# The first softplus stage in tile pairs over two token blocks, the second in halves, and a leaner attention front

## The chip, the core and the metric

The kernel runs on one core of one Trainium2 chip. The time is the device time of one execution, in microseconds (us). The engines are TensorE (PE, matmuls; PEld is its weight load), VectorE (DVE), ScalarE (ACT), GpSimd (POOL) and SyncE (SP, which issues most DMAs).

## The reference

A gated linear attention over 2 batches of 768 tokens (8 heads of 48) feeds a softplus layer, and that feeds four weighted ReLU experts:

```python
mag = np.sqrt(a_re * a_re + a_im * a_im)
scale = np.minimum(mag, 0.999) / (mag + 1e-06)
a_re_n, a_im_n = (a_re * scale, a_im * scale)
for t in range(S):
    new_re = ar * S_re - ai * S_im
    new_im = ar * S_im + ai * S_re
    kv = np.einsum('bhd,bhe->bhde', k[:, :, t], v[:, :, t])
    S_re, S_im = (new_re + kv, new_im)
    y[:, :, t] = np.einsum('bhd,bhde->bhe', q[:, :, t], S_re)
...
h = x @ w_in                                   # 1536 x 384 by 384 x 2048
g = np.maximum(h, 0.0) + np.log1p(np.exp(-np.abs(h)))
x = g @ w_out                                  # 2048 x 384
...
for e in range(E):                             # 4 experts, 384 -> 1024 -> 384
    h = np.maximum(x @ w1[e], 0.0)
    out += p[:, e:e + 1] * (h @ w2[e])
```

w_in and w_out come as 64-bit floats, the rest as 32-bit floats.

## The kernel before, in words

`fast_path` does the whole computation; `general_path` stands behind a flag and doesn't run on these inputs.

**Stages.** Twelve stages k, six for each batch: in a batch, stages 0 and 1 are the two halves (1024 columns each) of the softplus layer, stages 2 to 5 the experts. `ORDER` (line 40) gives their order; the last six are computed in another way (`FAST`) and aren't touched by the change. A matmul operand is split into a high and a low part (float32r), and a product takes three matmuls.

**A step.** `step` (line 366) takes a stage k, a block of tokens blk and one of eight column tiles f. `first` (236) runs nine h matmuls (line 232), and then, for softplus, ACT's Abs, Exp and Ln and DVE's line 250; in stage 0 two column tiles share one 512-wide tile. `second` (265), one step later, splits the result into two g tiles (lines 275 and 276, or 285 and 286). `third` (291), `LAG` = 3 steps later, runs nine y matmuls (314). Stage 0 has three blocks of 256 tokens (24 steps), the others two of 384 (16 steps). A block goes through all eight f before the next. At the last f of a block the sum is closed: stage 0 copies it to `Yt` (326), stage 1 adds it (331) and splits it into X (332, 333). PSUM has tiles by tag: `h` (2 banks), `a` (3), `y` (a tile of two banks) and `z` (1).

**Weights.** `weights` (160) loads the tiles A (first layer) and B (second layer) of four weight pairs a stage. In stages 0 and 1 a tile comes as two halves of 64-bit numbers: `load2` issues two loads on SP, `conv` runs `join` (69: lines 70 to 72 on DVE, which make 32-bit floats), `part` (179: ACT's 181 and DVE's 182) and stores the joined half to DRAM for batch 1 (line 200, on SP). Raw tiles have four buffers, slots nine (`NR`); three tiles of stage 1 have spare buffers (`early`), which later give their room to X of batch 1 (`swap`).

**Attention.** Six pairs of 128-token chunks, three a batch; the text counts pairs 1 to 6 and chunks 1 to 12 (the code counts n from 0). Batch 0 is pairs 1 to 3. For a pair: `squares` (543), `ratio` (549), `arctan`, `logmag` (558), then prefix sums by matmul (`prefix`, `wrap`, `level`), whose last row goes to the next chunk by a DMA on SP and an addition on POOL (`carry` 613, line 574), then `trig`. For a chunk (`s3_units`, 655): `decay` (653), `prep` (665), `turn` (transposes 674, copies 675), `score` (683, 684), `mix` (699), `state` (710, 714, 716) and `done`, which writes X (721, 722). Pairs 1 and 2 mix into bank z, pair 3 into an a bank. Block i of stage 0 needs pair i + 1.

**The order of the work.** Units are put at positions (`put`, 760), stage 0 at 0 to 24, stage 1 at 24 to 40, and are issued in order of position (`run`). A scheduler may still move instructions ahead where their inputs are ready. The weights of stage 0 stand at -5.2 + 1.6 n (n = 0 to 7: A and B of weight pair 1, then of 2, 3, 4), those of stage 1 at 8.3 + 2.3 n, later where a slot comes free later. `back(0)` (chunks 1 and 2) stands at -7.9 to -3.8, `back(1)` (3 and 4) at -0.7 to 6.3, `back(2)` (5 and 6) at 8.3 to 15.7 (lines 863 to 868).

```python
put([lambda k=k, blk=blk, f=f: step(k, blk, f) for blk in range(blks) for f in range(FH)], base[m], base[m + 1])
...
        pos, gap = -5.2 + 1.6 * n, 0.4
```

## Time and profile before

| | us |
|---|---|
| median of 3 runs | 737.89 |
| lowest and highest run | 735.72, 739.29 |
| span of the profiled execution | 736.2 |
| its own device time | not listed apart from the span |
| PE busy | 703.0 (95%) |
| DVE busy | 584.7 (79%) |
| ACT busy | 487.0 (66%) |
| POOL busy | 33.3 (5%) |

Busy is the time in which an engine has an instruction under way. Matmuls overlap, so that a listed matmul is longer than what it adds, and PE's busy time is an upper value. The chain that ended last is 70% PE, 10% DVE, 9% DMA and 8% ACT.

### The profile page before, as it was taken

Reading aid. Unit: us, or ns where it says so; the run is one execution under the profiler, and the core shown is the slowest. Engines: PE = TensorE matmul, PEld = TensorE weight load, DVE = VectorE, ACT = ScalarE, POOL = GpSimd, SP = SyncE. Lnnn points to the kernel's source line nnn. Section 1 sums busy time; section 2 is a strip of 40 time slices with the busy share of each in tenths; the row PEclk is TensorE's granted clock in tenths of the full one; section 3 lists DMA queues with packets and bytes.
Section 4 is the critical chain, followed back from the end, with each engine's and each line's share of the span. In section 5 each row is a group of like instructions: output and inputs, shape, how many; then the busy total and the mean of one; then the engine's idle time right before and its main releaser. Section 6 shows DMA issues by size and latency. Waiting matters only on the chain.

```text
span 736.2 us, 13313 instructions
## 1 busy us (share of the span) xinstructions
PE 703.0 (95%) x5171; PEld 676.2 (92%) x5171; DVE 584.7 (79%) x1150; ACT 487.0 (66%) x898; POOL 33.3 (5%) x31
## 2 busy tenths in 40 slices
PE   1688999999999999999999999999999999999996
PEld 0477899999899999999999999999999999999996
DVE  6999999955875854648888779988788899988963
ACT  7887886878896856345686666555556667666640
POOL 1132010000111011000000000000000000000000
PEclk9699999999999999999999999999999999999998
DMA  7655666721211420121022130213454445554501
GB/s 264 195 175 170 230 190 195 228 84 44 75 55 59 122 81 2 59 86 44 23 86 65 29 102 21 87 44 98 128 159 146 137 151 172 151 172 140 172 32 69
DMA packets 36486, 83.56 MB, mean 113 GB/s; under 512 B 4544, under 2 KB 13376, under 8 KB 36416
## 3 DMA queue, kind: packets, MB, share of 16 engines
q1 hardware_dynamic: 36128, 82.35, 35.5%
q8 instruction: 42, 0.69, 0.4%
q10 hardware_dynamic: 288, 0.30, 0.1%
q14 instruction: 28, 0.23, 0.1%
HBM read 73.95 MB, written 8.65 MB: 112 GB/s over the span
## 4 chain that ended last, share of the span: by engine, by line
PE 70%; DVE 10%; DMA 9%; ACT 8%; issue 2%; POOL 1%; SPq 0%; ACTq 0%; POOLq 0%; DVEq 0%
PE y L314 21%; PE h L232 18%; PE z L314 9%; PE px L425 7%; PE pv L425 3%; PE tp L674 2%; DMA rawB<-in_w_dram 2%; DMA chkw<-in_w_in_dram 2%; PE pc L425 2%; PE sp L683 2%; PE yps L699 2%; DMA chki<-in_a_im_dram 1%; PE ya L359 1%; PE sps L710 1%; DVE fA L72 1%
## 5 line engine op out<-in xcount | busy, mean ns | idle before, releaser
L232 PE MATMUL h<-X,A 128*128 128x384 f32 (+1 forms) x936 | 176.1, 329 | 2.5 <-ACT A L181 0.8
L232 PEld LDWEIGHTS h<-X,A 128*128 128x128 f32 x936 | 153.4, 188 | 5.8 <-issue 1.6
L314 PE MATMUL y<-B,g 128*128 128x384 f32 x744 | 150.0, 335 | 0.0
L314 PEld LDWEIGHTS y<-B,g 128*128 128x128 f32 x744 | 131.1, 188 | 0.5 <-issue 0.2
L314 PE MATMUL y<-g,B 128*128 128x384 f32 (+1 forms) x504 | 91.0, 315 | 0.3 <-ACT g L285 0.3
L314 PE MATMUL z<-B,g 128*128 128x384 f32 x372 | 84.7, 334 | 0.0
L314 PEld LDWEIGHTS y<-g,B 128*128 128x128 f32 x504 | 79.3, 189 | 1.9 <-ACT g L285 0.6
L314 PEld LDWEIGHTS z<-B,g 128*128 128x128 f32 x372 | 66.3, 188 | 0.0
L247 ACT ACTIVATE e<-h 128x384 f32<-128x384 f32 (+1 forms) x60 | 30.8, 513 | 37.3 <-PE h L232 36.3
L250 DVE SCALAR_TENSOR_TENSOR e<-h,e 128x384 f32<-128x384 f32 (+1 forms) x60 | 34.9, 581 | 21.0 <-ACT e L103 20.1
L255 DVE SCALAR_TENSOR_TENSOR g<-h,g 128x384 fp32r<-128x384 f32 x32 | 17.7, 554 | 28.2 <-ACT g L254 28.2
L103 ACT ACTIVATE e<-e,b_one 128x384 f32<-128x384 f32 (+1 forms) x60 | 38.2, 637 | 1.3
L103 ACT ACTIVATE e<-e 128x384 f32<-128x384 f32 (+1 forms) x60 | 32.8, 547 | 1.3
L425 PE MATMUL px<-X,sA 128*128 128x384 f32 x144 | 33.7, 339 | 0.0
L425 PE MATMUL px<-XC,sA 128*128 128x384 f32 x144 | 33.0, 337 | 0.1
L314 PE MATMUL z<-g,B 128*128 128x384 f32 x144 | 32.9, 335 | 0.0
L674 PE MATMUL tp<-ident,QK 128*96 128x128 f32 x192 | 27.3, 290 | 5.9 <-DVE QK L665 5.0
L674 PEld LDWEIGHTS tp<-ident,QK 128*96 128x96 f32 x192 | 22.4, 133 | 10.0 <-DVE QK L665 6.2
L254 ACT ACTIVATE g<-h 128x384 fp32r<-128x384 f32 x32 | 15.6, 487 | 21.3 <-PE h L232 21.1
L286 DVE TENSOR_TENSOR g<-e,g 128x384 fp32r<-128x384 f32 x48 | 26.7, 555 | 3.8 <-ACT g L285 3.0
L490 ACT CAST B<-rawB 128x768 fp32r<-128x768 f32 x24 | 20.0, 835 | 14.1 <-DMA rawB<-in_w_dram 7.6
L490 ACT CAST A<-rawA 128x384 fp32r<-128x384 f32 (+1 forms) x48 | 20.3, 457 | 11.6 <-DMA rawA<-in_w_dram 9.2
(204 smaller groups left out, 1424.4 us busy)
## 6 DMA issues: line engine op xcount, KB each, us to landing
rawA<-in_w_dram SPq DMA_DIRECT2D x32, 384.0 KB, 3.0
rawB<-in_w_dram SPq DMA_DIRECT2D x32, 384.0 KB, 3.1
rawA<-in_w_in_dram SPq DMA_DIRECT2D x16, 384.0 KB, 3.7
rawB<-in_w_out_dram SPq DMA_DIRECT2D x16, 384.0 KB, 3.8
chkw<-in_w_in_dram SPq DMA_DIRECT2D x16, 384.0 KB, 3.5
chkw<-in_w_out_dram SPq DMA_DIRECT2D x16, 384.0 KB, 3.3
qk<-in_qkv_dram SPq DMA_DIRECT2D x12, 384.0 KB, 3.3
v<-in_qkv_dram SPq DMA_DIRECT2D x12, 256.0 KB, 3.1
```

What stands on the lines that cost most here:

```text
L103: i = nc.scalar.activation(out_, in_, fn, **kw)
L232: nc.tensor.matmul(ps, wt[:, p, kk, o:o + P], XB[b][:, q, kk, tok], start=(n == 0), stop=(n == 3 * KT - 1))
L247: nc.scalar.activation(t, h, AF.Abs)
L250: nc.vector.scalar_tensor_tensor(t, h, 0.0, t, ALU.max, ALU.add)
L254: nc.scalar.activation(g[:, 0, :], h, AF.Relu)
L255: nc.vector.scalar_tensor_tensor(g[:, 1, :], h, 0.0, g[:, 0, :].bitcast(F32), ALU.max, ALU.subtract)
L286: nc.vector.tensor_tensor(g[:, 1, :], t, g[:, 0, :].bitcast(F32), ALU.subtract)
L314: mm = nc.tensor.matmul(ys[j], l_, r_, start=(opens and n == 0 and not mate), stop=(closes and n == 2), skip_group_check=k == 0)
L425: nc.tensor.matmul(ps, lt[:, p, li, :], rhs, start=(start and n == 0), stop=(stop and n == 2), skip_group_check=True)
L490: nc.scalar.copy(hi, src)
L674: nc.tensor.transpose(tp[:96, hh, :], src[:, hf * 4 + hh, :], ident)
L683: nc.tensor.matmul(sp[:, hh, :], kT[:, hh, :], qT[:, hh, :], start=True, stop=True)
```

## The change

- Stage 0 goes by `SEQ0`: weight pairs 1 and 2 over blocks 0 and 1, then these over block 2, then weight pair 3 over the three blocks, then 4. All three blocks are open at once: blocks 0 and 1 share the y and z banks, block 2 takes two of the three a banks.
- Stage 1 runs the first four f over both blocks, then the last four. It closes four times instead of twice; the first two closes only add to Y.
- Weight tiles of stages 0 and 1 stand at later positions, all in the nine slots; the spare buffers go, and X of batch 1 has its room from the start.
- Attention pairs 2 and 3 stand earlier: `back(1)` at -2.5 to 1.9, `back(2)` at 4.4 to 7.9, what leads to them at -8 to -2.6 and 0.2 to 4.2.
- The squares of pairs 2 and 3 are added on DVE instead of POOL.
- `ratio` loses the clamp of the slope; `logmag` keeps twice the log magnitude, with its small correction out of a biased Exp, and loses a scaling pass; `decay` halves the value in its Exp scale.

```diff
--- before.py
+++ after.py
@@ -40,6 +40,8 @@
 ORDER = (0, 1, 2, 3, 6, 7, 4, 5, 8, 9, 10, 11)
 AT = {k: m for m, k in enumerate(ORDER)}
 FAST = ORDER[6:]
+SEQ0 = ([(blk, 2 * j + i) for j in range(2) for blk in range(2) for i in range(2)] + [(2, f) for f in range(4)]
+        + [(blk, 2 * j + i) for j in range(2, 4) for blk in range(3) for i in range(2)])
 HALF = 4
 NORM_SPREAD = 2.0 ** 14
 
@@ -84,8 +86,7 @@
     att_ctx = ExitStack()
     att = att_ctx.enter_context(tc.tile_pool(name="att", bufs=1))
     psum = ctx.enter_context(tc.tile_pool(name="psum", bufs=1, space=PSUM))
-    early_ctx = ExitStack()
-    early = early_ctx.enter_context(tc.tile_pool(name="early", bufs=1, side="right"))
+    xb = ctx.enter_context(tc.tile_pool(name="xb", bufs=1, side="right"))
 
     NOSYNC = mybir.DependencyInfo(mybir.DependencyClass.NoSync, mybir.DependencyReason.DATA)
     tabs = {"load": None, "since": []}
@@ -129,6 +130,7 @@
     b_hpi = column("b_hpi", math.pi / 2.0)
     b_one = column("b_one", 1.0)
     b_tiny = column("b_tiny", 1e-37)
+    b_2eps = column("b_2eps", math.log(2e-6))
     b_mid = column("b_mid", -(2.0 ** 30))
     pr = const.tile([P, NTOK // P, NE], F32, name="pr")
     psm = const.tile([P, NTOK // P, 1], F32, name="psm")
@@ -201,11 +203,12 @@
 
         return [load2, lambda: conv(0), lambda: conv(1)]
 
-    XB = [xa.tile([P, 2, KT, S], F32R, name="X0"), None]
+    XB = [pool.tile([P, 2, KT, S], F32R, name=f"X{i}") for i, pool in enumerate((xa, xb))]
     Yt = [None]
     acc = {}
     home = [ac, None]
-    ps_y = [None]
+    ps_y = {}
+    opener = {}
     h_pair = [None]
     g_t = {}
     t_t = {}
@@ -292,31 +295,37 @@
         s = k % 6
         g = g_t.pop((k, blk, f))
         wt = W[k, f // 2 * 2 + 1]
-        nf = HALF if k in FAST else FH
+        nf = HALF if k in FAST or k == 1 else FH
         opens, closes = f % nf == 0, f % nf == nf - 1
         b, c0, nch, tok, TB = span(k, blk)
         nj, width = (KT, TB) if s < 2 else (nch, DM)
         if opens:
-            yt = psum.tile([P, 2, 512], F32, tag="y", name=f"y{k}_{blk}_{f}", bufs=1)
-            if k == 0:
-                ps_y[0] = [yt[:, j // 2, j % 2 * 256:j % 2 * 256 + 256] for j in range(nj)]
-            else:
+            lower, upper = slice(0, 256), slice(256, 512)
+            if k == 0 and blk == 2:
+                ya, yb = (psum.tile([P, 512], F32, tag="a", name=f"y{nm}{k}_{blk}", bufs=3) for nm in "ab")
+                ps_y[blk] = [ya[:, lower], ya[:, upper], yb[:, lower]]
+            elif k or blk == 0:
+                yt = psum.tile([P, 2, 512], F32, tag="y", name=f"y{k}_{blk}_{f}", bufs=1)
                 zt = psum.tile([P, 512], F32, tag="z", name=f"z{k}_{blk}_{f}", bufs=1)
-                ps_y[0] = [yt[:, 0, :width], yt[:, 1, :width], zt[:, :width]]
-        ys = ps_y[0]
+                if k == 0:
+                    for i, third_ in enumerate((lower, upper)):
+                        ps_y[i] = [yt[:, i, lower], yt[:, i, upper], zt[:, third_]]
+                else:
+                    ps_y[blk] = [yt[:, 0, :width], yt[:, 1, :width], zt[:, :width]]
+        ys = ps_y[blk]
         for j in range(nj):
             for n, (p, q) in enumerate(((0, 0), (0, 1), (1, 0))):
                 if s < 2:
                     l_, r_ = wt[:, q, f % 2, j * P:(j + 1) * P], g[p] if k == 0 else g[:, p, :]
                 else:
                     l_, r_ = g[:, p, j * P:(j + 1) * P], wt[:, q, f % 2, :]
-                mate = k == 0 and j == 1
+                mate = {(0, 1): (0, 0), (1, 1): (1, 0), (2, 1): (2, 0), (1, 2): (0, 2)}.get((blk, j)) if k == 0 else None
                 mm = nc.tensor.matmul(ys[j], l_, r_, start=(opens and n == 0 and not mate),
                                       stop=(closes and n == 2), skip_group_check=k == 0)
                 if opens and n == 0:
                     if mate:
-                        behind(mm, opened)
-                    opened = mm
+                        behind(mm, opener[mate])
+                    opener[blk, j] = mm
         if not closes:
             return
         if s == 0:
@@ -329,6 +338,8 @@
                 u = Yt[0][:, j, tok]
                 hi, lo = (XB[b][:, i, j, tok] for i in range(2))
                 nc.vector.tensor_tensor(u, ys[j], u, ALU.add)
+                if f < FH - 1:
+                    continue
                 nc.scalar.copy(hi, u)
                 nc.vector.tensor_tensor(lo, u, hi.bitcast(F32), ALU.subtract)
         else:
@@ -544,7 +555,7 @@
         R, I, T1, T2 = (wide(t, sl) for t in st[n])
         nc.scalar.activation(T1, R, AF.Square)
         nc.scalar.activation(T2, I, AF.Square)
-        (nc.vector if n == 0 else nc.gpsimd).tensor_tensor(T2, T1, T2, ALU.add)
+        (nc.vector if n < 3 else nc.gpsimd).tensor_tensor(T2, T1, T2, ALU.add)
 
     def ratio(n, sl):
         R, I, T1, T2 = (wide(t, sl) for t in st[n])
@@ -553,14 +564,12 @@
         nc.vector.tensor_tensor(R, R, T1, ALU.mult)
         nc.vector.scalar_tensor_tensor(R, R, 2.0, T1, ALU.subtract, ALU.mult)
         nc.vector.tensor_tensor(I, I, R, ALU.mult)
-        nc.vector.tensor_scalar(I, I, SLOPE_MAX, -SLOPE_MAX, ALU.min, ALU.max)
 
     def logmag(n, sl):
         T1, T2 = wide(st["z0"][1] if n == 0 else st[n][2], sl), wide(st[n][3], sl)
         act(T2, T2, AF.Ln, bias=b_tiny)
-        act(T1, T2, AF.Exp, scale=-0.5)
-        nc.vector.tensor_scalar(T2, T2, 0.5, LOG_CAP, ALU.mult, ALU.min)
-        nc.vector.scalar_tensor_tensor(T2, T1, -1e-6, T2, ALU.mult, ALU.add)
+        act(T1, T2, AF.Exp, scale=-0.5, bias=b_2eps)
+        nc.vector.scalar_tensor_tensor(T2, T2, 2.0 * LOG_CAP, T1, ALU.min, ALU.subtract)
 
     def arctan(n):
         I = wide(st[n][1], slice(0, 2))
@@ -608,7 +617,7 @@
         if cc == CB - 1:
             col = stats[96:128, 2 + b:3 + b]
             nc.vector.tensor_reduce(col, dlam[96:128, :], AX.X, ALU.min)
-            nc.vector.tensor_scalar(col, col, -LAM_MIN, None, ALU.add)
+            nc.vector.tensor_scalar(col, col, -2.0 * LAM_MIN, None, ALU.add)
 
     def carry(n, c):
         dth, dlam = (t[:, c, :] for t in st_out(n))
@@ -648,8 +657,8 @@
         qk = st["in", n, c][0]
         lam = st_out(n)[1][:, c, :]
         dec = att.tile([P, 2, HD], F32, tag="dec", name=f"dec{n}_{c}")
-        act(dec[:, 0, :], lam, AF.Exp)
-        act(dec[:, 1, :], lam, AF.Exp, scale=-1.0)
+        act(dec[:, 0, :], lam, AF.Exp, scale=0.5)
+        act(dec[:, 1, :], lam, AF.Exp, scale=-0.5)
         nc.vector.scalar_tensor_tensor(flat(qk), flat(dec), DECAY_MAX, flat(qk), ALU.min, ALU.mult)
 
     def s3_units(n, c):
@@ -803,9 +812,6 @@
 
     def slot(shape, dt, nm):
         return wp.tile(shape, dt, tag="w", name=nm, bufs=NR)
-
-    def spare(shape, dt, nm):
-        return early.tile(shape, dt, tag=nm, name=nm)
 
     def lag_out(k):
         return lambda: (second(*pipe[-1]) if pipe else None)
@@ -836,21 +842,20 @@
                 pos = need - 9
                 fast_events.append((pos, need, last, k, n))
             continue
-        blks = 3 if k == 0 else 2
-        put([lambda k=k, blk=blk, f=f: step(k, blk, f) for blk in range(blks) for f in range(FH)], base[m], base[m + 1])
+        seq = SEQ0 if k == 0 else [(blk, f + i) for f in ((0, HALF) if k == 1 else (0,)) for blk in range(2)
+                                   for i in range(HALF if k == 1 else FH)]
+        put([lambda k=k, blk=blk, f=f: step(k, blk, f) for blk, f in seq], base[m], base[m + 1])
         for n in range(8):
             if k == 0:
-                pos, gap = -5.2 + 1.6 * n, 0.4
+                pos, gap = (-5.2, -4.2, 1.0, 2.2, 8.2, 10.0, 12.5, 14.5)[n], 0.4
             elif k == 1:
-                pos, gap = 8.3 + 2.3 * n, 0.6
+                pos, gap = 16.5 + (2.4 * n if n < 4 else 2.6 + 1.6 * n), 0.6
             else:
                 pos, gap = base[m - 1] + 1 + 1.7 * n, 1.5
-            in_early = k == 1 and n in (2, 3, 4)
-            if not in_early:
-                if len(ring) >= NR:
-                    pos = max(pos, ring[len(ring) - NR] + 0.1)
-                ring.append(base[m + 1] - FH + 2 * (n // 2) + 1 + (LAG if n % 2 else 0))
-            for i, u in enumerate(weights(k, n, spare if in_early else slot)):
+            if len(ring) >= NR:
+                pos = max(pos, max(ring[:len(ring) - NR + 1]) + 0.1)
+            ring.append(base[m] + max(i for i, (blk, f) in enumerate(seq) if f == n // 2 * 2 + 1) + (LAG if n % 2 else 0))
+            for i, u in enumerate(weights(k, n, slot)):
                 events.append((pos + gap * i, len(events), u))
     for pos, need, last, k, n in sorted(fast_events):
         pos = max(pos, ring[len(ring) - NR] + 0.1)
@@ -862,17 +867,11 @@
             events.append((at, len(events), u))
     put(back(0), -7.9, -3.8)
     put([lambda: logmag(1, both)] + s2_units(1) + [lambda: s1_load(2), lambda: squares(2, both), lambda: ratio(2, both)]
-        + [excursion(lambda: trig(1), lambda: arctan(2))], -8, 0)
-    put(back(1), -0.7, 6.3)
-    put([lambda: logmag(2, both)] + s2_units(2) + [excursion(lambda: trig(2))], 1.3, 7.5)
-    put(back(2), 8.3, 15.7)
-
-    def swap():
-        early_ctx.close()
-        xb = ctx.enter_context(tc.tile_pool(name="xb", bufs=1, side="right"))
-        XB[1] = xb.tile([P, 2, KT, S], F32R, name="X1")
-
-    put([swap], base[2] + 3.5, base[2] + 4)
+        + [excursion(lambda: trig(1), lambda: arctan(2))], -8, -2.6)
+    put(back(1), -2.5, 1.9)
+    put([lambda: logmag(2, both)] + s2_units(2) + [excursion(lambda: trig(2))], 0.2, 4.2)
+    put(back(2), 4.4, 7.9)
+
     put([load_probs], base[2] + 1, base[2] + 2)
     b0, b1 = base[2] + 5.5, base[4] + 4.5
     w_ = (b1 - b0) / 3
```

## Rows read from the trace of the kernel before

**Rows 1.** The page, part 2: busy tenths in 40 slices of the span

```profile
PE   1688999999999999999999999999999999999996
...
DVE  6999999955875854648888779988788899988963
...
PEclk9699999999999999999999999999999999999998
```

**Rows 2.** Table by stretch: length; busy of PE, PEld, DVE, ACT, POOL; clock; DMA

```profile
38.00:83.00 45.00, 39.53 (x607) 33.16 (x602) 44.15 (x75) 36.75 (x64) 11.07 (x8) 1.00 0.58 182
83.00:144.00 61.00, 60.72 (x615) 58.34 (x616) 58.25 (x118) 47.72 (x90) 2.44 (x1) 1.00 0.65 206
144.00:200.00 56.00, 55.30 (x312) 53.64 (x311) 35.01 (x61) 48.59 (x92) 2.63 (x2) 1.00 0.25 77
```

**Rows 3.** The chain of waits in order of time: start, length, what

```profile
65.29 2.06 DVE fA L72
...
94.06 1.76 PE tp L674 x16
...
97.66 0.29 PE gs L260
97.94 0.89 PE sp L683 x8
...
102.68 1.02 PE sps L710 x48
...
113.89 1.95 PE yps L699 x64
...
118.18 1.08 PE h L232 x9
...
138.69 1.56 PE h L232 x9
...
142.96 1.08 PE y L314 x9
```

**Rows 4.** PE in order of time: start, length, instructions [idle before <- what ended it]

```profile
26.97 1.94 PE L674 MATMUL tp<-ident,QK 128*96 128x128 f32 x8 [3.78 <-DVE QK L665]
...
31.13 3.27 PE L674 MATMUL tp<-ident,QK 128*96 128x128 f32 x13
...
35.83 2.10 PE L683 MATMUL sp<-qT,kT 96*128 96x128 f32 x16
...
40.75 0.81 PE L593 MATMUL pf<-im,trik 128*128 128x384 f32 x2
...
56.66 1.96 PE L674 MATMUL tp<-ident,QK 128*96 128x128 f32 x16 [1.21 <-DVE QK L665]
...
64.91 1.52 PE L314 MATMUL y<-g,B 128*128 128x256 f32 x9
```

**Rows 5.** DVE, POOL and ACT in order of time, 12 to 15 us

```profile
12.91 2.04 DVE L555 TENSOR_TENSOR im<-im,re 128x384 f32<-128x384 f32 x1
...
12.44 2.09 POOL L547 TENSOR_TENSOR t<-t,t 128x768 f32<-128x768 f32 x1 [10.71 <-ACT t L546]
...
14.57 0.94 ACT L103 ACTIVATE t<-t,b_tiny 128x768 f32<-128x768 f32 x1 [1.02 <-POOL t L547]
```

**Rows 6.** DVE in order of time, 61 to 83 us

```profile
61.55 0.68 DVE L276 TENSOR_TENSOR g<-e,g 128x512 fp32r<-128x512 f32 x1
62.15 0.55 DVE L182 TENSOR_TENSOR A<-fA,A 128x384 fp32r<-128x384 f32 x1
62.62 0.35 DVE L70 TENSOR_SCALAR fA<-rawA 128x384 int32<-128x384 int32 x1
62.89 0.95 DVE L653 SCALAR_TENSOR_TENSOR qk<-dec,qk 128x768 f32<-128x768 f32 x1
...
82.49 0.56 DVE L722 TENSOR_TENSOR X<-yps,X 128x384 fp32r<-128x384 f32 x1
```

**Rows 7.** DVE in order of time at the first close of stage 1

```profile
168.84 1.02 DVE L331 TENSOR_TENSOR Y<-y,Y 128x384 f32<-128x384 f32 x2 [0.18 <-PE y L314]
```

## The prediction

> **What bounds the kernel now.** I began with the page's slices [rows 1]: TensorE (PE) is busy nine tenths or more in every slice from the fifth (74 us) on, and its holes lie in the first four, where VectorE (DVE) is the fuller. So only the start of the program can give time. The table by stretch [rows 2] says it in numbers: from 38 to 83 us DVE is busy 44.15 of 45.00 us and PE 39.53; from 83 to 144 us PE is busy 60.72 of 61.00, with DVE at 58.25. After 144 us DVE has room (35.01 of 56.00).
>
> PE's busy column flatters it, as matmuls overlap, so I priced its work by back-to-back pieces of the chain of waits [rows 3]. An attention chunk takes 1.76 us of transposes, 2 x 0.89 of scores, 1.95 of mixing and 1.02 of state, 6.5 in all. A step of stage 0 is nine first-layer (h) matmuls, 1.08, and nine second-layer (y) ones, 1.08; an h step of stage 1 is 1.56; a column sum is 0.29. Two prefix matmuls take 0.81 [rows 4].
>
> By 38.0 us 21 transposes (chunk 1 and five of chunk 2) and the 16 scores of chunk 1 are done [rows 4]. Left until chunk 4 is written to X: half a mix and the state of chunk 1, 2.0; chunk 2 less five transposes, 6.0; chunks 3 and 4, 13.0; 12 prefix matmuls of pairs 2 and 3, 4.8; and, in the order of the change, four h steps, 4.3: **30.1 us**. After that: chunks 5 and 6 without a last state, 12.0; the 20 other h steps and all 24 y steps of stage 0, 47.5; three column sums, 0.9; the three h steps of stage 1 that lie among them, 4.7: **65.1 us**. The last y of stage 0 ends at 144.0 [rows 3], so after 38.0 PE has 106.0 us for 95.2 us of work: 10.8 us are idle, nearly all that there is to win. The chain of waits in that stretch goes through joins, as in the 2.06 us pass of [rows 3].
>
> **The change part by part.**
>
> *The start.* The squares of pair 2 go from POOL to DVE; the clamp and a scaling pass go everywhere. The POOL square takes 2.09 us; the DVE multiply that runs beside it takes 2.04, and ACT waits 1.02 for the square [rows 5]; another two-input pass of that size takes 0.55 [rows 6]. DVE now pays 0.87 for the square (a 768-wide pass, 0.95, less the overlap of 0.08 that the others show [rows 6]); it gets back the 1.5 of the collision and, of pairs 1 and 2, four scalar passes of 0.27 and one of twice the width, 1.6. So attention starts earlier by 0 (if another chain covers it) to 2.2 us; I take 1.0, ACT's wait, since the table load and the angles stand behind it in ACT's queue. With pair 3's squares POOL's queue loses a second job ahead of its row additions; DVE's 0.87 for it and the passes dropped there cancel. The Trainium skill (Perfetto Trace Analysis, Optimizing Scalar/DVE Operations) speaks against this move: with DVE saturated, work may be offloaded to ScalarE or even GpSimd, though the read port that GpSimd and DVE share might undo that. By that rule alone the two squares cost DVE 1.7 us, bring nothing, and the forecast would be 2.7 us later; the 2.04 beside the 0.55 makes me go by the row.
>
> *The order of the joins.* A weight tile's join is two halves of a scalar pass, 0.27, and three two-input passes, 0.47 each from start to start [rows 6]: 3.4 us. Before, the six tiles of weight pairs 2 to 4 stand among chunks 3 and 4 (positions -2.0 to 6.8, the chunks at -0.7 to 6.3); after, two of them do (1.0 to 3.0), and four follow from 8.2. So 10 to 14 us of DVE work (three tiles or four) leave a stretch of 45 us in which DVE was 98% busy. By DVE alone chunk 4 would be written at 37.0 + 31 to 35 = 68 to 72 us; now it is 83.0 (L722, [rows 6]). By PE alone, full from 37.0, it is 37.0 + 30.1 = 67.1. I take **T = 71**, nearer to the DVE bound as DVE was the fuller engine; PE then idles 3.9 us before T, where now it idles 5.5 by its busy column. The joins' loads and stores go with them on SP's queue, so the row DMAs of chunks 3 to 5 have fewer ahead of them; I take no gain for that.
>
> *The z bank.* A third of the outputs of blocks 0 and 1 now lies in bank z, which pairs 1 and 2 use for mixing. So no y step can start before chunk 4 is read out; before, the first y steps run at 64.91, amid chunks 3 and 4 [rows 4]. PE's filler up to T is the four h steps counted above (the g tiles hold two pairs), and the rest comes after T. Block 2 takes two of the three a banks, but from position 11, after pair 3 (which ends at 7.9): nothing while that order holds; else each chunk of pair 3 runs its banks singly, at worst its 6.5 us bare, 13.
>
> *The sum on PE.* After T there are 65.1 us of work and, I take, 1.0 idle (0.3 of 61 by the busy column [rows 2]): stage 0's last y ends at 71 + 66.1 = 137.1 instead of 144.0, 6.9 earlier.
>
> *The later joins.* Twelve tiles, from weight pair 3 of stage 0 to the end of stage 1, stand between positions 8 and 32, where PE has 16 x 2.16 + 8 x 3.14 = 59.7 us. DVE has 12 x 3.4 = 40.8; softplus passes, eight pairs of 2 x 0.60 and eight steps of 2 x 0.47, 17.1; two splits for stage 2, 1.7; one half close, 1.4; in all 61. That is 102%, but three of the tiles are first needed at 34 to 37, and now PE stays at 60.72 of 61 beside a DVE at 95% [rows 2]. I take 0; at worst 5.5 (rival 2). Dropping the spare tiles costs nothing, as slots come free from position 9 on; without that cover, one join, 3.4.
>
> *Stage 1 in halves.* Two closes become four. The adds of a close take 0.51 each [rows 7], and the next y step waits for them; an h step of 1.56 lies between. Covered by it they cost nothing; bare, 1.5 for each of two new closes. I take 0.7 in all.
>
> The sum is -6.9 + 0.7 = **-6.2 us**. The profiled execution's own device time isn't listed apart from its span of 736.2; the three runs have a median of 737.89, 1.7 above the span, and the change touches nothing in that. So 737.9 - 6.2 = **731.7 us**.
>
> **The rivals.**
> 1. *Slower: the z bank holds the y steps back, and chunk 4 comes no earlier.* For it: the way to chunk 3 also runs through ACT's table switches, row DMAs and POOL, and the second slice has PE's clock at six tenths [rows 1]. Against: what ends the wait before chunk 3's transposes is DVE's QK [rows 4]. With T still at 83.0 the end is 83.0 + 66.1 = 149.1, 5.1 later; with the halves 743.7. It decides at T = 77.2, where the gain is zero. The Trainium skill (Perfetto Trace Analysis, Matmuls) wants independent groups to rotate through PSUM banks, so that one is read out while the next computes; two blocks in one bank go against that, and no run here shows its price.
> 2. *The joins come back late.* DVE's 61 and the next pair's three ratio passes with its POOL collision (4.1) meet 59.7: 5.4 us of PE waits in stages 0 and 1, 737.1. For it: the 102%. Against: the due positions.
> 3. *Positions hardly bind.* The scheduler reorders, joins of weight pairs 3 and 4 fill DVE ahead of their place, and T is about 76: end 142.1, 736.7 with the halves. For it: a DVE without gaps in that stretch [rows 2]. Against: the four raw buffers let only two tiles be loaded ahead.
> 4. *PE full from 37.0.* T = 67.1, end 133.2, gain 10.8 less 0.7: 727.8. DVE's 98% stands against it.
>
> **How the numbers follow.** A measurement of this kernel can tell about 0.5%, 3.7 us, from no change. Forecast (T from 68 to 75): 0.52; rivals 1 and 2: 0.12 each; rival 3: 0.10; rival 4: 0.14. Faster, under 734.2: 0.50 of the forecast, rival 4, 0.02 of rival 2: 0.66. Slower, over 741.6 (T over 81): 0.10 of rival 1. Within: the other 0.24. The range goes from 726.5 (rival 4 with the upper early shift) to 738.5 (rivals 2 and 3 with the halves at 1.5 to 2); it leaves out rival 1 and a few hundredths below.
>
> **What would show it.** Right: chunk 4 is written (L722) near 71 us, PE is busy nine tenths from the fourth slice on, the first y follows right behind that write, the last y of stage 0 ends near 137, and no PE wait stands at stage 1's closes. Wrong: that write after 77; y steps waiting for it with PE idle; matmuls of stages 0 and 1 waiting for A or B tiles after 100 us; transposes waiting for an a bank.

## The result: slower by 0.6%, all of it lost by 150 us

The changed kernel takes a median of 742.35 us (740.6 to 744.22, 6 runs) beside 738.02 us (735.72 to 739.55, 6 runs) for the kernel before: a ratio of 1.0063, 95% interval 1.0048 to 1.0079. The forecast of 731.7 us and its range up to 738.5 are missed, on the other side. The profiled execution took 743.14 us, with a span of 741.3.

The page's slices of the changed kernel, which answer to [rows 1]:

```profile
PE   2788899899999999999999999999999999999997
...
DVE  6899899865776773656989789988888889988963
...
PEclk9599999999999999999999999999999999999999
```

A slice is 18.5 us. PE now has holes up to the fifth slice (to 93 us) and again in the eighth (130 to 148), where before it was full from the fifth on; DVE still shows nine tenths in the third, fourth, sixth and seventh. The table by stretch, with the stretches of [rows 2], of the changed kernel (length; busy of PE, PEld, DVE, ACT, POOL; clock; DMA):

```profile
38.00:83.00 45.00, 37.80 (x563) 32.22 (x553) 41.68 (x73) 34.49 (x59) 9.25 (x7) 1.00 0.57 177
83.00:144.00 61.00, 56.48 (x582) 53.73 (x582) 57.68 (x110) 46.19 (x86) 2.59 (x1) 1.00 0.63 196
144.00:200.00 56.00, 53.11 (x309) 52.31 (x309) 34.29 (x62) 46.43 (x90) 0.00 (x0) 1.00 0.23 70
```

DVE did get lighter, and PE idles more: 7.2 us instead of 5.5 up to 83 us, and 4.5 instead of 0.3 in the next 61. The clock column is 1.00 in all three stretches, as it was before, so a lower clock is no part of the loss in this execution. Line numbers have grown by 2 to 11: L72 is here the first pass of a join, which was line 70. The events that the forecast named, in DVE's order of time (start, length, instruction, [idle before <- what ended it]):

```profile
24.27 0.96 DVE L674 TENSOR_TENSOR QK<-qk,re 128x768 f32<-128x768 f32 x1
...
70.27 0.36 DVE L72 TENSOR_SCALAR fB<-rawB 128x384 int32<-128x384 int32 x1 [1.09 <-DMA moe_weights<-fA]
...
71.48 0.55 DVE L731 TENSOR_TENSOR X<-yps,X 128x384 fp32r<-128x384 f32 x1
...
84.61 0.69 DVE L279 TENSOR_TENSOR g<-e,g 128x512 fp32r<-128x512 f32 x1 [2.54 <-ACT g L278]
...
86.53 0.96 DVE L674 TENSOR_TENSOR QK<-qk,re 128x768 f32<-128x768 f32 x1
...
146.76 0.36 DVE L72 TENSOR_SCALAR fB<-rawB 128x384 int32<-128x384 int32 x1 [2.48 <-DMA moe_weights<-fA]
```

Chunk 4 is written (L731) at 71.48, done by 72.0: 11 us earlier than in [rows 6], as forecast. But chunk 5's QK pass comes only at 86.53, and two joins (L72) stand waiting for a store to DRAM. PE in order of time after chunk 4 is written:

```profile
72.09 1.10 PE L235 MATMUL h<-X,A 128*128 128x256 f32 x7 [1.30 <-DVE X L731]
73.02 0.28 PE L263 MATMUL gs<-g,one_r 128*128 128x256 f32 x1
73.14 0.81 PE L602 MATMUL pf<-im,trik 128*128 128x384 f32 x2
...
75.58 0.76 PE L323 MATMUL y<-g,B 128*128 128x256 f32 x5
...
80.67 2.41 PE L235 MATMUL h<-X,A 128*128 128x256 f32 x18 [0.73 <-DVE e L253]
84.62 0.39 PE L263 MATMUL gs<-g,one_r 128*128 128x256 f32 x1 [1.54 <-ACT g L278]
...
88.41 2.02 PE L683 MATMUL tp<-ident,QK 128*96 128x128 f32 x16 [1.13 <-DVE QK L674]
...
102.87 0.86 PE L708 MATMUL yps<-A,v 128*32 128x128 f32 x24 [1.09 <-DVE A L693]
...
147.64 1.83 PE L235 MATMUL h<-X,A 128*128 128x384 f32 x9 [1.89 <-DVE e L253]
...
150.02 0.52 PE L323 MATMUL yb<-g,B 128*128 128x256 f32 x3
```

Waits for DVE and ACT now stand behind chunk 4's write, where PE before had 0.3 us idle in 61 [rows 2]. Stage 0's last y ends at 150.5 instead of 144.0 [rows 3], 6.5 us later. From there to the end of the span it is 590.8 us, and 592.2 before; in the 20 profiled kernels of this study it is 589.7 to 592.7. Whatever the change does to the time, it does before that y.

ACT shows what pair 3's attention waited for:

```profile
67.28 0.52 ACT L626 ACTIVATE tail<-im 32x384 f32<-32x384 f32 x1
...
74.16 0.51 ACT L183 CAST B<-fB 128x384 fp32r<-128x384 f32 x1 [2.52 <-DVE fB L74]
74.58 0.58 ACT L609 ACTIVATE im<-pf,b_magic 128x384 f32<-128x384 f32 x1
...
79.67 1.28 ACT L98 ACT_TABLE_LOAD   x1
80.97 0.94 ACT L104 ACTIVATE re<-re,b_hpi 128x768 f32<-128x768 f32 x1
81.81 0.83 ACT L104 ACTIVATE im<-im 128x768 f32<-128x768 f32 x1
82.66 1.28 ACT L98 ACT_TABLE_LOAD   x1
83.95 0.62 ACT L278 CAST g<-e 128x512 fp32r<-128x512 f32 x1
```

POOL, with the row addition in between:

```profile
71.44 0.99 POOL L583 TENSOR_TENSOR im<-rows,im 1x384 f32<-1x384 f32 x1 [10.89 <-DMA rows<-tail]
```

Pair 3's first prefix ends in the tail row at 67.28; that row travels by DMA to POOL, whose row addition runs at 71.44; the second prefix runs on PE at 73.14; ACT rounds it at 74.58, behind a cast that waited for a join; the angles sit between two table loads from 79.67 to 83.94. In that excursion the g cast of a step that was ready to be rounded has to wait, and the decays come behind it. Until 86.5 there is no attention to run, and the steps at hand stand behind the same ACT queue.

### The profile page after: what moved, and what is told of

Same layout as the page of the kernel before. It is cut to its first block, busy times and chain, and to the rows that moved or that the text cites. A ratio compares the mean times of both kernels' runs of the same rounds, so it can differ in the third digit from the quotient of the medians.

```text
span 741.3 us, 13309 instructions
## 1 busy us (share of the span) xinstructions
PE 701.3 (95%) x5171; PEld 675.0 (91%) x5171; DVE 584.5 (79%) x1145; ACT 488.9 (66%) x898; POOL 29.5 (4%) x29
## 4 chain that ended last, share of the span: by engine, by line
PE 73%; DVE 9%; ACT 9%; DMA 6%; issue 2%; POOL 0%; SPq 0%; DVEq 0%; ACTq 0%
PE y L323 22%; PE h L235 16%; PE z L323 11%; PE px L436 8%; PE pv L436 4%; PE pc L436 3%; PE tp L683 2%; PE yps L708 2%; ACT L98 2%; PE sp L692 1%; ACT t L104 1%; DMA moe_weights<-fA 1%; DMA moe_weights<-fB 1%; DMA chkr<-in_a_re_dram 1%; DMA chkw<-in_w_in_dram 1%
## 5 line engine op out<-in xcount | busy, mean ns | idle before, releaser
L235 PE MATMUL h<-X,A 128*128 128x384 f32 (+1 forms) x936 | 174.0, 327 | 4.5 <-DVE e L253 2.6
L323 PE MATMUL y<-g,B 128*128 128x384 f32 (+1 forms) x384 | 74.8, 325 | 1.0 <-ACT g L288 1.0
L323 PEld LDWEIGHTS y<-g,B 128*128 128x128 f32 x384 | 64.0, 189 | 1.8 <-ACT g L288 1.3
L323 PE MATMUL z<-g,B 128*128 128x384 f32 (+1 forms) x192 | 41.7, 323 | 0.0
L323 PEld LDWEIGHTS z<-g,B 128*128 128x128 f32 x192 | 33.0, 188 | 0.0
```

What stands on the lines that cost most here:

```text
L235: nc.tensor.matmul(ps, wt[:, p, kk, o:o + P], XB[b][:, q, kk, tok], start=(n == 0), stop=(n == 3 * KT - 1))
L323: mm = nc.tensor.matmul(ys[j], l_, r_, start=(opens and n == 0 and not mate), stop=(closes and n == 2), skip_group_check=k == 0)
```

## The experiments

The table has, for every kernel, when chunk 4's write starts, PE's idle time (length less PE's busy column) from 38 to 72, 72 to 90 and 90 us to the end of stage 0's last y, PE's busy time from 38 us to that end, the end, and the ratio to the kernel before. "New" is the changed kernel; all but the three named "before" are edits of it. All columns but the ratio come from one profiled execution, whose time lies up to 2.7 us from the median of its kernel (e2 and e8 2.7 and 2.5 under it, e10 2.6 over it), so ends compare only to within that and the ratio decides. In the six kernels whose clock column is 1.00 from 38 us to the end (before, new, e6, e8, e11, e15) the busy time is 98.1 to 100.3 us; in the others, at 0.96 to 0.98, it is 98.9 to 102.9.

| kernel | chunk 4 | idle to 72 | to 90 | to end | busy | end | ratio (95%) |
|---|---|---|---|---|---|---|---|
| before | 82.5 | 4.6 | 0.9 | 0.3 | 100.3 | 144.0 | 1 |
| new | 71.5 | 6.4 | 3.5 | 3.7 | 98.9 | 150.5 | 1.0063 (1.0048–1.0079) |
| e3 before, new front | 84.4 | 5.9 | 1.4 | 1.6 | 98.9 | 145.7 | 0.9998 (0.9983–1.0013) |
| e4 old front | 76.2 | 5.1 | 3.5 | 2.7 | 102.7 | 152.0 | 1.0106 (1.0088–1.0123) |
| e5 mixing in an a bank | 72.4 | 7.3 | 2.5 | 2.3 | 100.7 | 150.7 | 1.0089 (1.0061–1.0117) |
| e6 no halves | 71.7 | 6.6 | 4.1 | 2.8 | 98.7 | 150.2 | 1.0066 (1.0039–1.0093) |
| e1 four f buffers | 72.0 | 5.1 | 2.9 | 2.0 | 100.2 | 148.2 | 1.0040 (1.0022–1.0058) |
| e1b before, four f | 85.1 | 5.3 | 0.9 | 2.3 | 100.3 | 146.8 | 1.0053 (1.0037–1.0070) |
| e2 pair 3 early | 82.1 | 9.7 | 0.4 | 3.8 | 102.9 | 154.7 | 1.0189 (1.0162–1.0216) |
| e7 block 0 first | 74.0 | 4.4 | 4.9 | 2.6 | 100.9 | 150.8 | 1.0065 (1.0040–1.0089) |
| e8 pair 3 a little earlier | 73.3 | 5.4 | 1.0 | 3.7 | 98.1 | 146.2 | 1.0039 (1.0025–1.0054) |
| e9 = e8 + e1 | 74.6 | 4.7 | 0.3 | 2.2 | 100.7 | 145.7 | 1.0026 (1.0012–1.0040) |
| e10 = e9 + e7 | 76.9 | 5.2 | 0.6 | 1.6 | 102.8 | 148.3 | 1.0006 (0.9988–1.0023) |
| e11 = e10 + e5 | 76.5 | 5.0 | 1.4 | 2.6 | 98.3 | 145.3 | 1.0016 (1.0006–1.0026) |
| e12 = e10, prefixes later | 72.7 | 4.0 | 2.7 | 1.8 | 100.7 | 147.2 | 1.0060 (1.0039–1.0081) |
| e13 = e12 + e5 | 72.6 | 5.3 | 3.2 | 3.4 | 99.6 | 149.5 | 1.0059 (1.0039–1.0079) |
| e14 more steps | 74.6 | 6.4 | 2.7 | 3.9 | 101.4 | 152.4 | 1.0084 (1.0069–1.0100) |
| e17 their joins alone | 71.8 | 7.8 | 3.0 | 3.1 | 99.0 | 150.9 | 1.0091 (1.0064–1.0119) |
| e15 = e14 + e1 | 71.3 | 5.7 | 2.7 | 0.8 | 99.0 | 146.1 | 1.0006 (0.9994–1.0018) |
| e16 = e10 + e14 | 74.8 | 4.2 | 1.1 | 1.2 | 100.0 | 144.6 | 1.0007 (0.9990–1.0024) |

**Parts of the change.** First the leaner front alone, on the kernel before (e3: squares of pairs 2 and 3 on DVE, doubled logarithms, no clamp), and the new order alone (e4: those edits undone in the changed kernel).

Of the diff of e3, which e4 undoes:

```diff
-        (nc.vector if n == 0 else nc.gpsimd).tensor_tensor(T2, T1, T2, ALU.add)
+        (nc.vector if n < 3 else nc.gpsimd).tensor_tensor(T2, T1, T2, ALU.add)
...
-        nc.vector.tensor_scalar(I, I, SLOPE_MAX, -SLOPE_MAX, ALU.min, ALU.max)
```

> The kernel before with the leaner attention front alone (squares of pairs 2 and 3 on DVE, doubled log magnitudes, no clamp); order, joins and stages as before. If the front's saving reaches the end, as the prediction had it: chunk 1's rotation moves from 24.6 to about 24.0 us and the time is 1 us under before's 736.8 (735.8). If DVE's stretch from 38 to 83 us takes it up, or the squares cost DVE more than the collisions: no change or up to 2 us slower. Either way it is no part of the loss of 5 us if the order alone makes that.

> The kernel after with the old attention front (squares of pairs 2 and 3 on POOL, clamp, scaling pass): the new order alone. If the order makes the whole loss and the front gains 1 us: 743.4. If the front is what costs: 738 to 740.

The front alone brings nothing that can be measured (0.9998). The order alone costs 1.06%; within it the front is worth 0.4% (1.0106 to 1.0063, intervals apart). So the loss is in the order, with what else e4 keeps of the change (the halves of stage 1, the weights' positions).

The mixing of pairs 1 and 2 in an a bank (e5), and stage 1 block by block with one close for each (e6; the order of its steps goes back with the line shown):

```diff
-            yps = psum.tile([P, 512], F32, tag="z" if n < 2 else "a", name=f"yps{n}_{c}", bufs=1 if n < 2 else 3)
+            yps = psum.tile([P, 512], F32, tag="a", name=f"yps{n}_{c}", bufs=3)
...
-        nf = HALF if k in FAST or k == 1 else FH
+        nf = HALF if k in FAST else FH
```

> The kernel after, with the mixing of pairs 1 and 2 in an a bank instead of z, so that y steps needn't wait for chunk 4. Theory C (the z bank holds the y steps back): the first y steps run before 70 us, and the time falls by 3 to 6 us, to 736 to 739. Theories A and B: no gain; the three a banks are fuller, so chunk 4 is a little later and the time 742 to 745.

> The kernel after, with stage 1 going through all eight column tiles of a block before the next, as before the change, everything else as after it. If the halves cost what was predicted for them, 0.7 us: 741.7. If they pay for themselves because weight tiles come late for a block-wise stage 1: the tiles of weight pairs 3 and 4 are then due four steps (12.6 us) earlier, and PE waits for them: 745 to 750.

Neither changes the time: 1.0089 and 1.0066, both intervals overlap that of the change, and the last y stays at 150.7 and 150.2. Bank z and the halves are not where the time goes. In e5 two y matmuls run at 62.34 us and the next not before 79.01, 6 us behind chunk 4's write, though the mixing no longer holds bank z.

**The waits that the trace names.** A join writes its result to DRAM, and its f tile has two buffers, so the first pass of a later join waits for an earlier store. In the chain of waits of the changed kernel (start, length, what):

```profile
65.66 4.58 DMA moe_weights<-fA
...
74.16 3.47 DMA moe_weights<-fB
...
141.63 5.04 DMA moe_weights<-fA
```

Four buffers, in the changed kernel (e1) and in the one before (e1b); the f tiles also move from the pool `tmp` to `att`:

```diff
-            f = tmp.tile([P, HW], I32, tag="f", name=f"f{nm}_{h}", bufs=2)
+            f = att.tile([P, HW], I32, tag="f", name=f"f{nm}_{h}", bufs=4)
```

> The kernel after, with four buffers instead of two for the joined halves (f). Theory A (the joins stand behind their own stores): after chunk 4 is written at 72 us, DVE waits 1.09 us before, and 0.56, 1.01 and 2.48 us after, for the store of a joined half, and behind the last of these PE waits 1.89 us. With four buffers these DVE waits go: 2 to 5 us faster than the kernel after's 742.4, so 737 to 740. Theory B (pair 3 isn't ready) and theory C (the z bank) expect no more than 1 us, as PE's holes between 72 and 105 us stay.

> The kernel before with four buffers for joined halves, the control for the stores. Before, DVE waits for a store once, 0.5 us, and PE is full from 100 us on: within 1 us of 737.1. If the stores cost the kernel before as much (hidden in the order of the joins), 1.5 to 3 us faster; then they are no part of what the change lost.

In the changed kernel DVE's waits for stores vanish (two for loads stand there instead, 1.47 us the longer) and the last y ends 2.3 us earlier: 1.0063 becomes 1.0040 (the intervals overlap a little). In the kernel before, where DVE had waited for a store only once (0.5 us), the same edit costs 0.5%: up to 40 us eight halves have begun their join instead of six, chunk 4 is written 2.6 us later, and the last y ends 2.8 us later.

Next, pair 3's attention ahead of its place, by much (e2) and by a little with the angles kept back (e8):

```diff
-    put([lambda: logmag(2, both)] + s2_units(2) + [excursion(lambda: trig(2))], 0.2, 4.2)
+    put([lambda: logmag(2, both)] + s2_units(2) + [excursion(lambda: trig(2))], -2.6, 0.4)
```

```diff
-    put([lambda: logmag(2, both)] + s2_units(2) + [excursion(lambda: trig(2))], 0.2, 4.2)
+    put([lambda: logmag(2, both)] + s2_units(2), -1.2, 2.2)
+    put([excursion(lambda: trig(2))], 2.9, 3)
```

> The kernel after, with pair 3's log magnitude, prefixes and angles at -2.6 to 0.4 instead of 0.2 to 4.2. Theory B (after chunk 4 there is no attention to run, since pair 3's prefixes and the table switch for its angles end at 84 us): chunk 5's rotation (QK) moves from 86.5 us to about 78, the holes of PE between 72 and 88 (3.9 us) and part of the next 2.5 close: 3 to 6 us faster than 742.4, so 736 to 739. Theory A and C: within 1 us of 742.4, or a little slower, as chunk 4 is put back by the work moved ahead of it.

> The kernel after, with pair 3's log magnitude and prefixes at -1.2 to 2.2, its angles' table switch at 2.9 (0.2 to 4.2 in the kernel after; -2.6 to 0.4 in the earlier try, where ACT stood in the angles' table from 56.9 to 70.5 us waiting for the prefixes). Theory B: with the prefixes earlier and the switch not ahead of them, chunk 5's rotation comes at 80 to 83 us instead of 86.5, and the time falls by 2 to 4 us. If ACT's queue or DVE's order takes that back again: 742 to 746.

e2 went the other way, 1.9% over the kernel before. ACT in order of time shows a part of why:

```profile
56.94 1.28 ACT L98 ACT_TABLE_LOAD   x1
...
65.81 0.48 ACT L730 CAST X<-yps 128x384 fp32r<-128x384 f32 x1 [3.76 <-PE yps L708]
...
68.81 0.94 ACT L104 ACTIVATE re<-re,b_hpi 128x768 f32<-128x768 f32 x1
69.66 0.83 ACT L104 ACTIVATE im<-im 128x768 f32<-128x768 f32 x1
70.50 1.28 ACT L98 ACT_TABLE_LOAD   x1
```

The switch to the table of angles came at 56.94, long before the angles could be computed (68.81), and no exponential ran from then until 73.7. The switch is not all of it: PE's longest wait in 38 to 72 us, 2.47 before 54.40, is a prefix of pair 3 that stands in PE's queue and waits for POOL's row addition. e8 brings chunk 5's QK pass to 76.54 (from 86.53) and the idle time of 72 to 90 us from 3.5 to 1.0, and the last y 4.4 us forward, in an execution 2.5 us under its median: 1.0039, which still overlaps the change's interval. With four f buffers as well (e9) it is 1.0026, and this interval (1.0012 to 1.0040) lies clear of the change's (1.0048 to 1.0079): pair 3's lateness and the stores together make over half of the loss.

The order of the blocks (e7), and the sums of these edits (e9, e10, the second with the order of e7):

```diff
-SEQ0 = ([(blk, 2 * j + i) for j in range(2) for blk in range(2) for i in range(2)] + [(2, f) for f in range(4)]
+SEQ0 = ([(blk, f) for blk in range(3) for f in range(4)]
```

> The kernel after, but weight pairs 1 and 2 go over block 0, then block 1, then block 2; weight pairs 3 and 4 as after. Theory D (too little filler: by the order of the change the third and fourth step belong to block 1, which waits for chunk 4, so that PE has two h steps of filler until 72 us; block 0's own four steps are behind them): four h steps run before chunk 4 is written, and PE's idle time from 38 to 90 us, 9.9 us by the busy column in the kernel after, falls by 2 to 4: 738 to 740. If the filler isn't what lacks (pair 3 late, stores, z): within 1 us of 742.4.

> The kernel after with both: pair 3's prefixes at -1.2 to 2.2 and its table switch at 2.9, and four buffers for joined halves. If the two losses are separate (pair 3 late, 1.8 us; joins behind their own stores, 1.7 us), they add: 737.06 x 1.0063 - 3.5 = 738.2; if the stores are what gives back pair 3's gain (with the prefixes alone PE is idle 3.0 us of 106 to 130, in two waits that begin with a store of 4.2 to 4.4 us), more than add: 735 to 737. If they are the same loss seen twice: 740.

> The same with weight pairs 1 and 2 over block 0, then 1, then 2. If filler before chunk 4 counts once pair 3 and the stores are out of the way: 1 to 2 us under the run without it. If, as with this order alone, block 0's steps only move: within 1 us of it.

e7 gives PE four h steps to run before chunk 4 instead of two. The idle time up to 72 us falls by 2.0 and that of 72 to 90 rises by 1.4, the time stays: the steps were only moved. With all three edits the kernel equals the one before (1.0006).

**PE's queue, or the bank after all.** In e10 PE, in order of time, has the second prefixes of pair 3 in the middle of chunk 4's mixing, waiting for POOL:

```profile
69.16 0.41 PE L708 MATMUL yps<-A,v 128*32 128x128 f32 x2
71.54 1.65 PE L602 MATMUL pf<-im,trik 128*128 128x384 f32 x2 [1.97 <-POOL im L583]
72.97 1.49 PE L602 MATMUL pl<-t,tri 128*128 128x384 f32 x2
74.39 1.72 PE L708 MATMUL yps<-A,v 128*32 128x128 f32 x27
```

Behind that wait two prefix matmuls take 1.65 us, where they take 0.81 in [rows 4], and the granted clock of 72 to 90 us is 0.84. e12 puts the prefixes at -0.5 to 2.6; e11 and e13 move the bank, without and with that.

```diff
-    put([lambda: logmag(2, both)] + s2_units(2), -1.2, 2.2)
+    put([lambda: logmag(2, both)] + s2_units(2), -0.5, 2.6)
```

> The change with four f buffers and block 0 first, and pair 3's prefixes at positions -0.5 to 2.6 instead of -1.2 to 2.2 (its angles stay at 2.9 to 3). Before this edit the second prefix pair of pair 3 stood in TensorE's queue in the middle of chunk 4's mixing and held it 1.97 us for GpSimd's row addition, at half clock after it. Theory (TensorE's order puts work that isn't ready ahead of work that is): that wait goes, chunk 4 is written 2 to 4 us earlier (73 to 75), chunk 5's QK pass stays near 83, and the time is 0.2 to 0.5% below the kernel before (734 to 736.5). Rival (what is lost is a sum of DVE and ACT work that no position changes): the wait goes but the time stays within 0.2% of the kernel before.

> The change with four f buffers, block 0 first, pair 3's prefixes at -1.2 to 2.2, and the mixing of pairs 1 and 2 in an a bank instead of bank z. With block 0 first, TensorE has four h steps and, if bank z is free, y steps of block 0 to fill its waits with before chunk 4 is read out. Theory that bank z does hold y steps once there are g tiles for them: y matmuls run before 72 us, TensorE's busy time from 38 to 90 us rises by 1 us or more, and the time is 0.15 to 0.4% below the kernel before. Theory that the bank costs nothing, as with the bank alone changed: 0.998 to 1.003 of the kernel before, and no y before chunk 4 beyond one or two.

> Both edits at once: four f buffers, block 0 first, pair 3's prefixes at -0.5 to 2.6, mixing of pairs 1 and 2 in an a bank. If both the place of the prefixes and bank z cost time by themselves, this is the fastest, 0.3 to 0.8% below the kernel before (732 to 736). If neither does, 0.998 to 1.003 of it, and the order's early chunk 4 is worth nothing here even with every wait named so far eased.

The wait went, chunk 4 came 4.2 us earlier (72.7), and the time rose to 1.0060: the theory fell. PE's busy time rose by 1.2 us up to 72 us and fell by 2.0 from there to 90, where e10 had the lower clock (0.84; 1.00 in e12). Why e12 is 0.5% slower than e10, with intervals apart, the runs don't show. The bank gives nothing in either.

**Do the steps run out?** In the changed kernel the last h step of blocks 0 and 1 ends at 83 us and but for two matmuls no other runs until chunk 6 is written at 105.6. e14 makes weight pair 3 ready for them; e17 moves only its joins; e15 adds the four f buffers; e16 is e10 with these joins and the same twelve steps, block by block.

```diff
-        + [(blk, 2 * j + i) for j in range(2, 4) for blk in range(3) for i in range(2)])
+SEQ0 = ([(blk, 2 * j + i) for j in range(3) for blk in range(2) for i in range(2)] + [(2, f) for f in range(6)]
+        + [(blk, 6 + i) for blk in range(3) for i in range(2)])
...
-                pos, gap = (-5.2, -4.2, 1.0, 2.2, 8.2, 10.0, 12.5, 14.5)[n], 0.4
+                pos, gap = (-5.2, -4.2, 1.0, 2.2, 4.6, 6.4, 12.5, 14.5)[n], 0.4
```

> The change, with one more weight pair ready before block 2: the joins of weight pair 3 stand at positions 4.6 and 6.4 instead of 8.2 and 10.0, and stage 0's order is weight pairs 1, 2, 3 over blocks 0 and 1 (twelve steps), then pairs 1 to 3 over block 2, then pair 4 over all three. Theory (TensorE runs out of steps): between chunk 4's write (72.0 us) and chunk 6's (105.6) lie 33.6 us, and the work that the change allows there is six h steps, eight y steps, two attention chunks and a prefix pair, 6.5 + 8.6 + 12.0 + 1.5 = 28.6; the last h step of blocks 0 and 1 ends at 83 us, and no other runs until chunk 6 is written. Four more steps give 8.6 us of work, so idle time between 72 and 106 us falls from 4.8 to 2.5 us or less, the last y of stage 0 ends 2 to 5 us earlier (145 to 148), and the time is 738 to 740.5. Rival (work is there, but each matmul waits for its own softplus, table or QK pass): idle time stays within 1 us of 4.8 and the time within 0.2% of the change's.

> The change, with only the joins of weight pair 3 at positions 4.6 and 6.4 (was 8.2 and 10.0), and the order of the steps as in the change. It gives VectorE the earlier joins and TensorE no more steps. Theory that TensorE lacks steps: no gain, 741.5 to 745, and no h step between 83 us and chunk 6's write. Theory that it is the joins' stores and lateness behind position 8 that cost: 738 to 741.

> Twelve steps before block 2 and the joins of weight pair 3 at 4.6 and 6.4, with four f buffers. Theory that steps are lacking, and that the waits of the joins for their stores are a cost of their own: the two gains add, 736 to 738.5, last y of stage 0 at 142 to 146. Rival: within 0.2% of the change with four f buffers alone (739.99).

> Everything that eased a named wait: twelve steps before block 2 with the joins of weight pair 3 at 4.6 and 6.4, four f buffers, pair 3's prefixes at -1.2 to 2.2 and its angles at 2.9 to 3, block 0 ahead of block 1. Theory that steps are lacking: faster than the kernel before by 0.2 to 0.7% (732 to 736), since the same kernel with eight steps before block 2 equals the one before. Rival: 0.998 to 1.004 of the kernel before.

Alone, more steps bring nothing (1.0084; 5.1 us idle from 72 to 106, where it was 4.8), nor do the earlier joins alone (e17, 1.0091), and so the lack of steps is not the cause by itself; chunk 4 came 3.1 us later, and DVE still waited for stores up to 1.56 us. With four f buffers as well, the end is at 146.1 and the ratio 1.0006, where four buffers alone gave 1.0040 (0.9994 to 1.0018 beside 1.0022 to 1.0058). The steps pay only where the buffers are there too. e16, with everything, comes to the kernel before and not below it. The table by stretch, from 38 us to the last y: the kernel before,

```profile
38.00:144.04 106.04, 100.28 (x1222) 91.55 (x1218) 102.44 (x191) 84.50 (x153) 13.51 (x9) 1.00 0.62 196
```

the changed kernel,

```profile
38.00:150.54 112.54, 98.92 (x1175) 90.40 (x1166) 102.84 (x191) 84.47 (x153) 11.84 (x8) 1.00 0.59 183
```

and e16:

```profile
38.00:144.57 106.57, 100.03 (x1189) 92.17 (x1182) 100.63 (x188) 83.68 (x153) 14.37 (x8) 0.98 0.65 201
```

PE's busy time is the same within 1.4 us in the three, and 98.1 to 102.9 in all 20 kernels. So the end is 38 us, some 100 (give or take 2.4, in part by the clock) and the idle time. The time of chunk 4's write is not in that sum: 71.3 (e15) ends at 146.1, 82.5 (before) at 144.0, and 72.7 (e12) at 147.2.

## Why the prediction was wrong

- **The start** was forecast 1.0 us earlier, 0 to 2.2. The first QK pass starts at 24.27, 0.36 earlier than before (24.63). The collision did go (the im multiply takes 0.55 instead of the 2.04 of [rows 5], the square 0.96 on DVE), and e3 and e4 give it 0 to 0.4%. The Trainium skill (Perfetto Trace Analysis, Optimizing Scalar/DVE Operations) says that offloading from a saturated DVE may make sense, and that between DVE and GpSimd it might not help, as they share a read port. By the first half alone the squares should have cost; neither run shows a cost.
- **The order of the joins** held in its total and not in its parts. DVE did 44.15 us of work up to chunk 4's write before (from 38 to 83 us, [rows 2]) and does 32.37 now (38 to 72 us): 11.8 us less, forecast 10 to 14. But the joins make only 8.0 of it. DVE's work on the tiles fA and fB (first fA, then fB: busy of DVE, of ACT; clock; DMA), in the kernel before,

```profile
38.00:83.00 45.00, 14.78 (x21) 3.08 (x6) 1.00 0.58 182
38.00:83.00 45.00, 7.96 (x16) 1.84 (x4) 1.00 0.58 182
```

  and in the changed one:

```profile
38.00:72.00 34.00, 9.27 (x16) 2.02 (x4) 1.00 0.51 159
38.00:72.00 34.00, 5.47 (x11) 1.20 (x3) 1.00 0.51 159
```

  Nine halves began there before and six now, so one and a half tiles left, not three or four; a half took 2.2 to 2.5 us, not the 1.7 of its shortest passes. Joins of weight pair 3, whose place is behind chunk 4, begin at 63.76: to that extent the third rival was right.
- **T** was 72.0, forecast 71, and that is in part luck: the forecast had 30.1 us of work on PE and 3.9 idle in those 34 us, the run had 27.6 and 6.4. Work that was to run before T, two h steps and four prefix matmuls, was missing, and PE idled in its place.
- **The z bank**: the first y of stage 0 but for one matmul is at 75.58, behind chunk 4, as said, but not for that bank: with the mixing out of it (e5) they come no earlier (79.01). Only two h steps ran before T, not four, since the third and fourth are block 1's and need chunk 4 itself; and as the y matmuls of a step are issued three steps after its h (`LAG`), I take it that this order holds them, which was not tested apart. The Trainium skill (Perfetto Trace Analysis, Matmuls) wants independent matmul groups to rotate through PSUM banks; no run here separates the two blocks that share one, so this rule's price stays unknown.
- **The sum on PE** is the step that failed: "After T there are 65.1 us of work and, I take, 1.0 idle". From 72.0 to 150.5 PE had 71.3 us of busy time and 7.2 idle. Against 137.1 the end moved by 1.0 (T) + 1.9 (16 h matmuls not run before) + 1.5 (the second prefixes of pair 3, which I had put before T) + 6.2 (idle) + 2.8 (the rest, which I put down to the busy column instead of back-to-back pieces) = 13.4. The 1.0 idle was read off the old order, where pair 3's attention and steps of weight pairs 3 and 4 lay ready when chunk 4 was written. Of the 7.2 us, 3.5 lie before 90 us, and 3.0 more are two waits behind joins on DVE: 1.09 before 102.87, and 1.89 before 147.64, where the join itself waited for a store. The change leaves neither of the two: pair 3 goes through a DMA, POOL, ACT and two table loads until 86.5, and the joins of the later weight pairs come later.
- A step ahead of it is wrong too: "10.8 us are idle, nearly all that there is to win". That came from 95.2 us of work priced at the shortest pieces. No kernel of the 20 did that work in under 98.1 us of busy time; in the one before it was 100.3, and 5.8 were idle. And in every order 4.0 to 9.7 us stayed idle up to 72 us, with DVE relieved or not. So of idle time 5.8 less 4.0, some 1.8 us, was to be had in these orders, and some 2 us more of busy time (98.1 in e8 beside 100.3): by this estimate under 4 us, not 6.9, and no order had both.
- **The later joins** were taken at 0. They wait for their own stores (2.48 us at 146.76, and behind it PE for 1.89): about 1.7 us by e1 (0.23% of 738), with intervals that overlap a little. I had counted DVE's passes and not the time that a store holds the buffer.
- **Stage 1 in halves**, taken at 0.7: e6 shows no difference, and no long wait of PE stands at the closes.
- **The rivals.** The first gave 743.7 and is near the time measured (742.35), but by luck: T was not 83 and the bank is not the cause. The second, joins that come late, is real at about a third of its 5.4 us. None said that PE idles after an early chunk 4; it was the missing one.

What stays open: which of DVE's, ACT's and PE's queues would have to be ordered otherwise for the idle time up to 72 us to fall under 4 us. Nothing tried does it, and no version beat the kernel before. That more f buffers slow that kernel because its joins run ahead of attention is a reading of the trace, not tested. Open too is why e12, with its wait gone and chunk 4 earlier, is slower than e10. Dropping the spare tiles was not tried alone; from the last y of stage 0 on, where stage 1 uses its tiles, the changed kernel loses nothing (590.8 us beside 592.2).

## What to carry to other kernels

An engine's stretch was worth nearer to its idle time by the busy column (5.8 us here) than to the difference from its shortest pieces (10.8); take the first as the ceiling of what a reordering can give, give or take what the busy time itself moves from order to order. Before pricing an earlier event, list what is ready to run right behind it: an event that comes 11 us earlier is worth nothing when its successors wait for another chain. A step that is moved later takes its buffers and stores with it, so price the time that a store holds a tile.

## What was not expected of the hardware

- A store of a joined half to DRAM held its buffer for 1.8 to 5.0 us from issue to landing (median 2.9 of 32 stores in the changed kernel), beside some 1.7 us of DVE for a half. With two buffers DVE waited for a store four times up to 150 us, 0.56 to 2.48 us each; with four (e1) not once. In the kernel before, with stores of 1.8 to 4.1 us, it waited once, 0.5 us.
- The granted clock fell behind some waits of PE. Its mean from 72 to 90 us is 0.81 in e2 and e5 and 0.84 in e10, part of the stretch (71 to 77 us in e10) at the lower level of 1.2 GHz. A wait of that length did not always bring it: in the changed kernel PE waits 2.43 us before 53.34 and the clock stays at 1.00. Nor is a fall in one profile shown to belong to its order: the mean over a whole run goes from 0.986 to 1.000 in runs of the kernel before. PE in order of time in e2: behind the wait, 16 score matmuls take 3.62 us, where they take 2.10 in [rows 4].

```profile
72.43 0.64 PE L683 MATMUL tp<-ident,QK 128*96 128x128 f32 x4 [2.07 <-ACT qT L684]
73.34 3.62 PE L692 MATMUL sp<-qT,kT 96*128 96x128 f32 x16
```

- More buffers can slow a kernel: four f buffers instead of two, in the other pool, cost the kernel before 0.53% (0.37 to 0.70).
